# Spectra scratch read in gather order, tables built on TensorE, and LayerNorm moved ahead of the tables, in a fused long-convolution and FFN kernel

## The chip, the cores and the metric

The kernel runs on one core of a Trainium2 chip. The metric is the device time in microseconds of one execution. A kernel's figure is the median of its runs. A run of one core is called slow when it lies more than 1.5% above the fastest of the same kernel. The profile comes from one profiled execution; its span is about 2 us shorter than the run's time.

## The reference, cut to what matters

```python
x  = A_q                                    # 1 x 2048 x 640, bf16
xn = layernorm(x)
# A: a 4-tap shift convolution, then a convolution as long as the sequence, per channel
k_shift = sum over 4 taps of shifted k * shift_k
kv = k_shift * v
y  = irfft(rfft(pad(kv)) * rfft(pad(ssm_k)))[:2048] + kv * ssm_D
s  = xn * y
# B: FFN, 640 -> 1728 -> 640
g  = silu(gelu(xn @ w1 + b1) @ w2 + b2)
# the output is x plus the product s * g
```

The output is x with a small product added. The tolerance of the comparison doesn't notice if the rows of the spectra are permuted. "Correct" is therefore no argument for a change of layout here.

## The kernel before

The long convolution is a two-stage DFT written as matmuls. Stage 1 transforms the filter (kT) and kv (v_all) and stores its results in two scratch tensors in DRAM, scrK and scrU. Stage 2 reads them back in a different order, so that the second index lies on the partitions. It transforms, multiplies the two spectra, transforms back (i1) and stores into scrC. The last stage (i2) reads scrC and finishes. The FFN's matmuls are interleaved with all this. Each engine has a fixed order of instructions.

```python
scrK = dram.tile([2, P * N2, H], BF16)      # likewise scrU, scrC; P = 128, N2 = 32, H = 320 (640 bytes)

def by_h(scr):    # how stage 1 stores and how the last stage reads
    return scr.rearrange("b (p h j) d -> p b h j d", h=2, j=NJ)      # 128 is outermost
def by_n2(scr):   # how stage 2 reads
    return scr.rearrange("b (k q) d -> q b k d", q=P)                # 128 is outermost

# stage 1 store (32 for scrK, 32 for scrU), out of 4 staging buffers
nc.gpsimd.dma_start(out=by_h(scr)[:, b, :, j, :], in_=o.v[:, b])

# conv_unit(b, u), 12 units: read both spectra, then DFT, product, pair sums, inverse DFT, store
nc.sync.dma_start(out=dst.v[:, 0:n].rearrange("p (k d) -> p k d", d=H), in_=by_n2(scr)[:, b, k0:k1, :])
...
nc.vector.tensor_tensor(out=q[:, r], in0=uu..., in1=ku..., op=ALU.mult)                         # prod
nc.vector.tensor_tensor(out=q[:, :, 0, 0], in0=q[:, :, 0, 0], in1=q[:, :, 1, 1], op=ALU.subtract) # comb
nc.vector.tensor_tensor(out=q[:, :, 1, 0], in0=q[:, :, 1, 0], in1=q[:, :, 0, 1], op=ALU.add)      # comb
...
nc.gpsimd.dma_start(out=by_n2(scrC)[:, b, k0:k1, :], in_=uin.v...)                              # store

# last stage, 8 reads of 640 KB
nc.sync.dma_start(out=cb.v, in_=by_h(scrC)[:, b, :, 4 * i:4 * i + 4, :])
...
# two tables: G is W transposed by four DMA transposes; the shift weights are a broadcast DMA of 640 KB
nc.sync.dma_start_transpose(out=G[:, 4*i:4*i+4, :], in_=W[:, 4*i:4*i+4, :]...)
nc.gpsimd.dma_start(out=wb, in_=wsh_v.to_broadcast([P, 2, 4, H]))
```

Of the kernel before, what the change touches and what calls it, by code (L numbers as in the profile page):

```python
# [9 lines left out]
F32 = mybir.dt.float32  # L10
# [3 lines left out]
ALU = mybir.AluOpType  # L14
# [57 lines left out]
class Plan:  # L72
# [3 lines left out]
    def op(self, kind, engs, fn, reads=(), writes=(), mods=(), hold=(), extra=(), size=0):  # L76
        o = Op()
        o.kind, o.engs, o.fn, o.size, o.i = kind, engs.split("|"), fn, size, len(self.ops)
        o.deps, o.allocs, o.bufs, o.after = set(extra), [], [], []
# [52 lines left out]
21s -20d 6p0 16s 10s -21g 12s -24d 25s 10d -13s 14d 2a -1d -23g 25a -28p1 4d 16s 13g -31g 45d -12s 11d 2d -50p0 54d  # L132
-55p1 56a 1d -38s -22p0 13a 135p20 -93g 1d 1d -33s 149p41 2p6 1d -115d 89p0 24d -23a -130s 147p02 2p6 55d -163g 107a
-20a 3g -151p0 41s 22d 113g -112p10 2p0 -69p2 45s 20d 108a -13p43 1a 1p6 1a 1g -94d -71p2 76d -4p3 -3a 106g -161a 60p0
-57d 58d 154d -156a -47s 64p00 6p1 134d 1d 1d 1d -141p2 5a -4a 153d -152p3 1a 11p4 128p60 6p21 -5a -69p63 1a 69g -129a
134d -73p2 -64p1 139p62 4d 1d -171d -47s 214a -136p4 134g -73a 76g -154a 9p5 9a 128p60 -132a 144d 1d -12a -186s 199d
7p21 -6p02 -199s 206a -147p4 -14p2 155a -152a -83g 84p3 152g -15g -126a 3p0 -84s 82p1 -11a 161d 1d 1d 1d 1d 14d -165a
143g -150p3 5a -16a 102p62 -45p40 1a -103s 149p0 1d -46p4 44a -16p61 2p0 -160s -20p2 151d -48a 59g 212p20 -335s 158g
-24p43 6a 2d -6p6 -181p3 382p0 -202a 2a 199a 2a -225g 46p42 2p6 -130d 1d 1d 307p11 -197g 17a -11p20 73d 14d 1d -93p41
94d 1d 100d -177a -11p6 191p0 -192a -5a -111g 1d -34s 151a 88d -202d 100g 25g -17p2 101p43 94a -305d 212a -101a 178p10  # L140
18a -341s 151g 11p62 2p4 161p0 -78g -8p20 -202s1 126a -123s 125a -130d 289a -73d 91d -175p63 2p4 71a -72a 2a -24g 106d
74a 2p11 -290s 134p21 81d 1d -80p6 -180d -28d 73s 127g 75g 14d -254s 255d -85g 158a -60d 61p0 -157a 2a 52p42 104a -61d
-173p20 131a 43d 1d -173p6 174d -97g 53g -131a 176d 13d 1d -111s 188d -296p11 8p0 16p2 155p43 -163p3 15a 1g 129p61
-160a 179a 1g 116d -145p42 143d -283p1 -79s 92a 137a -145a -8a 211d 1d 1d -69a 83d -73g -149p2 209d -210a -9p0 1a 149g
-11p60 12p43 -11a 114d -252p1 150a 262s1 -400p0 -8p3 284d -185s -90a 154p61 -36p42 -135p0 143g -138a 150g -19a 36a
-154p1 6p4 113g 36g -153p5 -11a -88s 314d 61d 1g -61d -235a 12a 6a 6a -4a 397p6 -205p20 221s0 -224p03 207s0 -119d -87a
66p40 -46p02 -17a 47d -75p21 26g 207a -140p5 -64g 87s0 -24a 77d -123d 1g -46a 169d 64p6 4p0 -187d 43a -360s 379d -111g
264s2 -151d 134s1 -14a -140d 145p2 1a -155p41 -83p63 236a -3d1 -215p20 -17a 1g 37p02 75s -95a 21a -20g 64a 1p5 31s
-75g 45a -80p61 228d -227a 232d 1d 1p20 2a -235g 157d -72p40 154p6 2p0 -7a -74d 1d 1g -121d 232s1 -231d 200a -214p23
59p5 153a -154a 77d 73g -133d -24d -50d 17p00 -51p62 169d -57s -77g -5p21 140d -118a 43p41 -64d 217d0 -195g -21g 217d  # L150
-156a -92a 95a -94g 248p0 2p2 10p6 -11a 2d 8s0 -164p5 75s1 91a -9d -156a -44p03 -6p20 66p40 60s -125d -37p61 43a 1g
1p02 198d -242d 45d 115s -58a 9p5 1a -26g 165p2 4p6 11s2 -14a 5p0 -136p4 -120g 255d -98d -444s 544a 25s0 -164p5 3a
121p62 -123a -3p0 167s3 -39a 22p4 2p2 -25a -119p1 -2p6 145a -15d2 6d 1d -214g 208d 16d -152a 143p42 10d1 -145a -2a
138d 10d -157p7 148a 10p0 2p2 10p4 -39g -130a 158d 2a 1d 1d 8a -173p6 1a -5p7 178p2 4p0 1d -130s -52a -73g 264s2 -13a
5p4 -4d0 5a 1d -31g 26d -187p6 199s1 -23p20 2a 15d 17s1 1s0 -187p7 153a -176a 24a -21p4 -2p5 -24d 27a 189p02 2d -17g
-176a 192a -135p61 168s0 -167a 139p4 2p2 -1d 11p0 1a -10d 1d2 -7g 8d -135p7 144p4 4p0 2p2 -149a 148d -183p61 179a 1d1
5a 9p4 -24p20 16d 7s2 -21d 38s2 -23d 8a -190p70 191p4 15s3 -40a -170a 180d 16d -24g 55s1 1s1 -29p2 2p0 -1a 2a -196p6
-1a 182p24 -180a 190d0 -196p7 202d -15a -180d 190d -9a 1g 14d -202a 209p0 2p2 -1d 5p4 -3a -220p60 211p20 10d2 1d 2a
-11d 12p4 26s0 -39a 14a -225a 1p7 233p2 2p0 -234a 233a 5p4 -204p6 190d 15d -4a 43s0 -29s0 -217p7 193d 41s2 -231a -2a
193p24 -15g 16a -189p0 1a 11p1 1a -475s 664p6 10p2 38s1 -21s2 -31d1 1d -9d 23a -203p4 1a -43d 235d 1d 1d 9p0 4p6 37s2  # L160
-35p2 -1d -4a -211p5 217a -258d 43p4 -1a 201p02 10d0 1d -210a -17p5 232d 8p6 -23a 38s3 -37a 23a -8d 9p0 -240p4 241a
-242a 11p2 222p60 -221a 188g 35a 8d2 -220p3 211d -217p2 227d -26g 27p06 -243a 245d -223a 212g 10a -283p31 55a 239p4
5p0 -7p6 -290p2 -1a 294d -10g 15d -7d -290a 299p4 -13p0 -285d 300p6 1d -15d -213p20 1a 1p3 224d 3s3 -19p6 1d -208a
239s2 -12p0 -226g 251s0 -19p4 1d 3d -250p21 241d -240a 252p6 6p4 -257p3 252d 24s3 -18d -12g -6d 19d 1s 1d 1s -34p0
42p6 1d -16d 9p4 -263a 271d -23s -256p20 2p3 258g 12d 8s -19s -25d -235a 8d 239s 27d -2d 11p6 6p4 -5d -282a 273s 12d
-39d 5s 35s -26s -259d 246s 36d -12s 13s -6d 1s 9d 3d 1s -285p21 2p3 -1a 2a 1d 278d 1s
# [3 lines left out]
def kernel(  # L170
# [23 lines left out]
    def by_h(scr):  # L194
        return scr.rearrange("b (p h j) d -> p b h j d", h=2, j=NJ)

    def by_n2(scr):
        return scr.rearrange("b (k q) d -> q b k d", q=P)

# [18 lines left out]
    rstd = sb.tile([P, NJ], F32, name="rstd")  # L218
    dD_row = sb.tile([1, D], BF16, name="dD_row")
# [37 lines left out]

    def evict(e, out_, in_):
        (nc.scalar.copy if e == "ACT" else nc.vector.tensor_copy)(out=out_, in_=in_)  # L259
# [20 lines left out]
    wb_b, dD_b, b1r_b, b1_b, id_b, bias_b, ones_b = (Buf() for _ in range(7))  # L280
# [16 lines left out]
    op("zero", "DVE", lambda e: nc.vector.memset(xtra[:, 0:D], 0.0), writes=[z_b])  # L297
# [5 lines left out]
    def iotas(e):  # L303
        for h in range(2):
            nc.gpsimd.iota(tok[64 * h:64 * h + 64, :], pattern=[[1, NJ]], base=16 * h, channel_multiplier=32,
                           allow_small_or_imprecise_dtypes=True)
        nc.gpsimd.iota(k4[:], pattern=[[4, NK1], [4 * NK1, 2]], base=1, channel_multiplier=0,
                       allow_small_or_imprecise_dtypes=True)
# [4 lines left out]
    def small1(e):  # L313
        g = nc.gpsimd
        g.iota(pint[:, 0:1], pattern=[[0, 1]], base=0, channel_multiplier=1)
        g.iota(smi[:, 0:32], pattern=[[1, 32]], base=0, channel_multiplier=0, allow_small_or_imprecise_dtypes=True)
        g.iota(smc[:, 0:64], pattern=[[8, 2], [0, 32]], base=72, channel_multiplier=0, allow_small_or_imprecise_dtypes=True)
        g.iota(smc[:, 64:192], pattern=[[8, 2], [-8, 2], [0, 32]], base=72, channel_multiplier=0,
               allow_small_or_imprecise_dtypes=True)
        g.memset(pcol[:, 1:2], 0.0)  # L320
        for r in range(2):
            g.memset(pcol[64 * r + 32:64 * r + 64, 1:2], -8.0)

    op("small1", "POOL", small1, writes=[sm_b])

    def small2(e):
        g = nc.vector
        g.tensor_single_scalar(out=pint[:, 0:1], in_=pint[:, 0:1], scalar=31, op=ALU.bitwise_and)
        g.tensor_copy(out=pcol[:, 0:1], in_=pint[:, 0:1])
        g.tensor_scalar(out=smi[:, 0:32], in0=smi[:, 0:32], scalar1=pcol[:, 0:1], scalar2=None, op0=ALU.mult)  # L330
        g.tensor_tensor(out=smc.rearrange("p (a b) -> p a b", b=32), in0=smc.rearrange("p (a b) -> p a b", b=32),
                        in1=smi[:, None, 0:32].to_broadcast([P, 6, 32]), op=ALU.add)
        g.tensor_scalar(out=smc[:, 0:64], in0=smc[:, 0:64], scalar1=pcol[:, 1:2], scalar2=None, op0=ALU.add)
        g.tensor_copy(out=smq, in_=smc)
        g.tensor_single_scalar(out=smq, in_=smq, scalar=31, op=ALU.bitwise_and)

    op("small2", "DVE", small2, writes=[sm_b])
    op("tabsin", "ACT", lambda e: nc.scalar.activation(out=tabs[:], in_=smq, func=ACT.Sin,
# [10 lines left out]
    def small_rows(e):  # L349
        nc.scalar.dma_start(out=b1_r[:], in_=b1_v)  # L350
        nc.scalar.dma_start(out=dD_row[:], in_=dD_v)
# [5 lines left out]
    for q in range(CH):  # L357
        load(lambda e, q=q: nc.sync.dma_start(out=x01[:, q, :], in_=x_v[:, q, :]), 160, writes=[x_b[q]])
# [409 lines left out]
```

## Time and profile before

| reading | value | view |
|---|---|---|
| time | 204.97 us (204.82 to 207.04) | three runs |
| TensorE (PE) busy | 175.4 of 202.4 us | page, part 1 |
| VectorE (DVE) busy | 172.3 us | page, part 1 |
| first FFN matmul | 21.2 us | timeline |
| first read of a scratch tensor | 75.2 us | timeline |
| 16 DMA engines, 10 to 40 us | 412 to 417 GB/s, 26 per engine | page, part 2 |

Here are the busy times of the page of the kernel before: busy time, share of the span and number of instructions of each engine.

```profile
span 202.4 us, 4736 instructions
PE 175.4 (87%) x1846; PEld 88.5 (44%) x1846; DVE 172.3 (85%) x301; ACT 138.4 (68%) x206; POOL 70.6 (35%) x103
```

The page's 40 slices of the span follow; one slice is 5.06 us. Each digit is a busy share in tenths, and the last line is what the DMA engines moved.

```profile
PE   4039887689999899799999699999999999999991
DVE  7399969949999989859987978989999999467993
DMA  6999999954599988969988999686959997486664
GB/s 180 352 412 417 413 412 416 416 194 129 164 225 178 357 346 256 224 158 292 236 253 227 192 328 198 200 250 213 297 129 357 283 368 251 131 216 185 231 237 171
```

The reader should see two things. TensorE does little in the first three slices and is nearly full after slice 10. And after slice 8 the DMA engines move less than the 412 to 417 GB/s that they reached before.

The chain of waits that ended last comes next: shares of the span, first by engine, then by line.

```profile
PE 47%; issue 17%; DMA 13%; POOL 13%; DVE 5%; ACT 3%; SPq 1%; POOLq 0%; ACTq 0%; DVEq 0%
PE ps L459 18%; PE ps L491 18%; DMA scrU<-mm 9%; POOL scrK L532 6%; POOL scrU L532 4%; PE ps L638 4%; DMA x<-in_x_dram 3%; PE ps L669 3%; PE ps L691 3%; ACT mm L259 2%; POOL rstd L422 2%; DVE mm L259 1%; DVE stats L415 1%; PE ps L524 1%; ACT L495 1%
```

The DMA issues of the scratch tensors (count, KB of each, median us from issue to landing) show what a read costs when all 16 engines work on it:

```profile
mm<-scrC SPq DMA_DIRECT2D x8, 640.0 KB, 6.9
v_all<-scrU SPq DMA_DIRECT2D x10, 480.0 KB, 4.6
k_all<-scrK SPq DMA_DIRECT2D x6, 480.0 KB, 6.4
```

In the timeline (start, duration, engine, line, operation) these are the group that begins with the first FFN matmul and the first read of a scratch tensor:

```profile
21.21 7.00 PE L459 MATMUL ps<-xnT,w_sb 128*128 128x512 bf16 x25 [1.04 <-ACT xnT L259]
75.23 0.39 SPq L621 DMA_DIRECT2D xtra<-scrK  x1
```

### The profile page before, as it was taken

The numbers are of one execution on the slowest core, as the hardware profiler recorded it, in microseconds if no ns is written. First come the engines' busy times: TensorE is split into PE (matmuls) and PEld (weight loads), VectorE is DVE, ScalarE is ACT, GpSimd is POOL, SyncE is SP. The second block draws the span as 40 slices with busy tenths as digits, with TensorE's granted clock in tenths as the row PEclk, the third lists the DMA queues.
The fourth block names the chain that finished last, engine by engine and source line by source line (L and its number), as shares of the span: only waits on it lengthen the run. The fifth ranks groups of instructions, "written<-read, shape, count | busy, mean of one in ns | idle before, by whom it ended". The sixth has DMA issues, their size and how long they took to land.

```text
span 202.4 us, 4736 instructions
## 1 busy us (share of the span) xinstructions
PE 175.4 (87%) x1846; PEld 88.5 (44%) x1846; DVE 172.3 (85%) x301; ACT 138.4 (68%) x206; POOL 70.6 (35%) x103
## 2 busy tenths in 40 slices
PE   4039887689999899799999699999999999999991
PEld 1015332235555333355555234435665444566660
DVE  7399969949999989859987978989999999467993
ACT  4635467576977696599687759998987999611110
POOL 7018314068977434342545603111111101306200
PEclk9999999999999999999999969999999999999999
DMA  6999999954599988969988999686959997486664
GB/s 180 352 412 417 413 412 416 416 194 129 164 225 178 357 346 256 224 158 292 236 253 227 192 328 198 200 250 213 297 129 357 283 368 251 131 216 185 231 237 171
DMA packets 41191, 53.09 MB, mean 262 GB/s; under 512 B 12817, under 2 KB 32818, under 8 KB 41170
## 3 DMA queue, kind: packets, MB, share of 16 engines
q1 hardware_dynamic: 35376, 36.41, 61.4%
q0 software_dynamic: 5648, 16.39, 24.7%
q8 instruction: 14, 0.23, 0.4%
q14 instruction: 7, 0.06, 0.1%
q10 hardware_dynamic: 146, 0.00, 0.0%
HBM read 31.95 MB, written 18.35 MB: 249 GB/s over the span
## 4 chain that ended last, share of the span: by engine, by line
PE 47%; issue 17%; DMA 13%; POOL 13%; DVE 5%; ACT 3%; SPq 1%; POOLq 0%; ACTq 0%; DVEq 0%
PE ps L459 18%; PE ps L491 18%; DMA scrU<-mm 9%; POOL scrK L532 6%; POOL scrU L532 4%; PE ps L638 4%; DMA x<-in_x_dram 3%; PE ps L669 3%; PE ps L691 3%; ACT mm L259 2%; POOL rstd L422 2%; DVE mm L259 1%; DVE stats L415 1%; PE ps L524 1%; ACT L495 1%
## 5 line engine op out<-in xcount | busy, mean ns | idle before, releaser
L459 PE MATMUL ps<-xnT,w_sb 128*128 128x512 bf16 (+1 forms) x280 | 68.9, 392 | 4.7 <-ACT mm L259 3.5
L491 PE MATMUL ps<-w_sb,hT 128*128 128x320 bf16 x448 | 65.9, 300 | 0.3 <-ACT hT L463 0.2
L491 PEld LDWEIGHTS <-hT 128*128 128x128 bf16 x448 | 41.8, 98 | 21.6 <-issue 5.8
L259 ACT CAST mm<-ps 128x640 bf16<-128x640 f32 x52 | 34.2, 698 | 23.1 <-PE ps L524 11.2
L459 PEld LDWEIGHTS <-w_sb 128*128 128x128 bf16 (+1 forms) x280 | 25.6, 100 | 41.5 <-issue 17.1
L463 ACT ACTIVATE hT<-ps,b_f 128x512 bf16<-128x512 f32 (+1 forms) x56 | 36.7, 697 | 8.1 <-PE ps L459 8.0
L532 POOL DMA_DIRECT2D scrU<-mm x32 | 22.3, 753 | 42.7 <-ACT mm L259 37.5
L259 ACT CAST v_all<-ps 128x960 bf16<-128x960 f32 (+2 forms) x34 | 30.3, 928 | 3.8 <-PE ps L669 2.3
L495 ACT ACTIVATE sl<-ps 128x320 bf16<-128x320 f32 x32 | 14.1, 445 | 21.5 <-PE ps L491 21.2
L680 POOL DMA_DIRECT2D scrC<-v_all x12 | 9.9, 826 | 49.1 <-ACT v_all L259 26.0
L532 POOL DMA_DIRECT2D scrK<-mm x32 | 23.4, 903 | 5.7 <-ACT mm L259 5.3
L524 PE MATMUL ps<-kT,W 64*128 64x320 bf16 x64 | 8.3, 338 | 11.8 <-DMA kT<-in_kT_dram 8.1
L524 PEld LDWEIGHTS <-W 64*128 64x128 bf16 x128 | 5.3, 97 | 25.9 <-issue 19.4
L698 DVE TENSOR_TENSOR xn<-ps,xn 128x640 bf16<-128x640 f32 x16 | 12.5, 816 | 4.1 <-PE ps L691 4.0
L259 DVE CAST v_all<-ps 128x960 bf16<-128x960 f32 (+2 forms) x12 | 12.2, 1014 | 4.3 <-PE ps L669 2.2
L259 DVE CAST mm<-ps 128x640 bf16<-128x640 f32 x12 | 9.6, 817 | 6.8 <-PE ps L524 5.9
L553 DVE TENSOR_TENSOR mm<-k_all,mm 128x2560 bf16<-128x2560 bf16 x8 | 11.9, 1485 | 0.2
L550 DVE TENSOR_TENSOR mm<-k_all,mm 128x2560 bf16<-128x2560 bf16 x8 | 11.9, 1486 | 0.1
L638 PEld LDWEIGHTS <-tabs 64*32 64x32 bf16 x704 | 7.6, 90 | 9.5 <-issue 8.4
L524 PE MATMUL ps<-v_all,W 64*128 64x320 bf16 x64 | 8.1, 302 | 2.3 <-DVE v_all L557 1.5
L651 DVE TENSOR_TENSOR k_all<-v_all,xtra 128x960 bf16<-128x960 bf16 x16 | 9.7, 652 | 0.3
L651 DVE TENSOR_TENSOR kT<-v_all,k_all 128x960 bf16<-128x960 bf16 x16 | 9.6, 650 | 0.1
(86 smaller groups left out, 199.7 us busy)
## 6 DMA issues: line engine op xcount, KB each, us to landing
scrK<-mm POOLq DMA_DIRECT2D x32, 160.0 KB, 4.8
scrU<-mm POOLq DMA_DIRECT2D x32, 160.0 KB, 5.0
mm<-scrC SPq DMA_DIRECT2D x8, 640.0 KB, 6.9
v_all<-scrU SPq DMA_DIRECT2D x10, 480.0 KB, 4.6
scrC<-v_all POOLq DMA_DIRECT2D x10, 480.0 KB, 4.2
k_all<-scrK SPq DMA_DIRECT2D x6, 480.0 KB, 6.4
kT<-in_kT_dram SPq DMA_DIRECT2D x4, 640.0 KB, 9.4
v_all<-in_v_dram SPq DMA_DIRECT2D x4, 640.0 KB, 14.7
```

What stands on the lines that cost most here:

```text
L259: (nc.scalar.copy if e == "ACT" else nc.vector.tensor_copy)(out=out_, in_=in_)
L459: nc.tensor.matmul(out=ps.v[0:M, :], lhsT=w1_sb[:, ft, t, 0:M], rhs=xnT_b[c].v[:, t, :], start=(t == 0), stop=(t == DT - 1))
L463: op("gelu", "ACT", lambda e: nc.scalar.activation(out=hT_b[c].v[0:M, ft, :], in_=ps.v[0:M, :], func=ACT.Gelu_apprx_tanh, bias=b1_f[0:M, f ...
L491: nc.tensor.matmul(out=ps.v[:, 0:H], lhsT=hT_b[c].v[0:M, ft, q * P:(q + 1) * P], rhs=w2_sb[0:M, ft, h * H:(h + 1) * H], start=(ft == 0), s ...
L495: op("silu", "ACT", lambda e, h=h, ps=ps: nc.scalar.activation(out=sl.v[:, h * H:(h + 1) * H], in_=ps.v[:, 0:H], func=ACT.Silu), reads=[ps ...
L524: nc.tensor.matmul(out=ps.v[:, h, 0:H], lhsT=W[r, j, :], rhs=src[r, b, j, :], start=True, stop=True)
L532: nc.gpsimd.dma_start(out=by_h(scr)[:, b, :, j, :], in_=o.v[:, b])
L550: op("kv2", "DVE", lambda e: tt(out=kt_t, in0=win(0, 2), in1=wbc(0, 2), op=ALU.mult), reads=kb + [wb_b], writes=[kvt_b], extra=[u for b in ...
L553: op("kv2", "DVE", lambda e: tt(out=kt_t, in0=win(2, 2), in1=wbc(2, 2), op=ALU.mult), reads=kb + [wb_b], writes=[kvt_b])
L638: nc.tensor.matmul(out=ps.v[32 * g:32 * g + 32, r, i * w:(i + 1) * w], lhsT=F2[i][64 * r:64 * r + 64, :], rhs=part(src.v[64 * r:64 * r + 6 ...
L651: nc.vector.tensor_tensor(out=q[:, r], in0=uu[:, r, :, None, :].to_broadcast([P, 2, 2, w]), in1=ku[:, r, None, :, :].to_broadcast([P, 2, 2 ...
L698: nc.vector.tensor_tensor(out=xv, in0=ps.v[:, :, 0:H], in1=xv, op=ALU.mult)
```

## The change

There are four intents. The stage 2 reads shall move 3840 contiguous bytes at a time where they moved 640. Work shall go from DMA to TensorE: the transposes of G, and the broadcast of the shift weights. The first LayerNorm shall run ahead of the table building, so that the FFN starts earlier. And the stores of stage 1 shall be spread over two queues, with the pair sums partly on GpSimd (POOL).

The diff, cut to its core (the order tables, the declarations and the mechanics of the head are left out):

```diff
     def by_h(scr):
-        return scr.rearrange("b (p h j) d -> p b h j d", h=2, j=NJ)
+        return scr.rearrange("b (k c h j) d -> c k b h j d", c=4, h=2, j=NJ)
+    def put_h(scr):
+        return scr.rearrange("b (h j p) d -> p b h j d", ...)
+    def get_n2(scr):
+        return scr.rearrange("b (n c k) d -> c n b k d", n=N2, c=4)
...
-                nc.gpsimd.dma_start(out=by_h(scr)[:, b, :, j, :], in_=o.v[:, b])
-        op("s1st" + kind, "POOL", st, ...)
+                dma(e)(out=put_h(scr)[:, b, :, j, :], in_=o.v[:, b])
+        op("s1st" + kind, "POOL|SP", st, ...)
...
-            nc.sync.dma_start(out=dst.v[...], in_=by_n2(scr)[:, b, k0:k1, :])
+            nc.sync.dma_start(out=dst.v[...], in_=get_n2(scr)[:, :, b, k0:k1, :])
...
-            op("comb", "DVE", comb, ...)
+            op("comb", "DVE|POOL", comb, ...)
...
-        op("cst", "POOL", lambda e: nc.gpsimd.dma_start(out=by_n2(scrC)[:, b, k0:k1, :], ...
+        op("cst", "POOL|SP", lambda e: dma(e)(out=by_n2(scrC)[:, b, k0:k1, :], ...
...
-            op("cin", "SP", lambda e: nc.sync.dma_start(out=cb.v, in_=by_h(scrC)[:, b, :, 4 * i:4 * i + 4, :]),
+                for h in range(2):
+                    nc.sync.dma_start(out=cb.v[:, h], in_=by_h(scrC)[:, :, b, h, 4 * i:4 * i + 4, :])
...
-        op("gtr", "SP", ... nc.sync.dma_start_transpose(out=G[...], in_=W[...]))         # x4
+                nc.tensor.transpose(out=ps.v[:].bitcast(BF16)[...], in_=W[:, CH * i + j, :], identity=ident[:])  # x16
-    op("wb", "POOL", ... nc.gpsimd.dma_start(out=wb, in_=wsh_v.to_broadcast([P, 2, 4, H])))
+        op("wbm", "PE", ... nc.tensor.matmul(out=ps.v[:], lhsT=<row of ones>, rhs=wrow_f[...]))   # x5
...
+    ln_group([0, 1])                    # now ahead of the tables
+    ln_group([2, 3], (2,))
```

In `get_n2` the row number is (n c k): c steps less far than n and still stands outermost in the pattern. So c and n can't be merged into one dimension of 128, and the pattern begins with a dimension of size 4. The same holds for c and k in the new `by_h`.

## The prediction

> **What bounds the kernel now.** The page's span is 202.4 us; PE is busy 175.4 us (87%), DVE 172.3, ACT 138.4. In the chain of waits the FFN matmuls lead (L459 18%, L491 18%). PE time is lost mainly in two places. In the head, the timeline shows the first FFN matmul at 21.2 us: the third x tile lands only at 10.1 us, because kT, k and w1 loads are mixed with x; LayerNorm, transposes and evictions follow. In the slices from 5 to 40 us the 16 DMA engines are 90 to 99% busy at 412 to 417 GB/s, so 26 GB/s per engine. Then about 10 us go between 28 and 46 us (waits for scratch stores; the chain gives "DMA scrU" 9%). From 115 us on PE is nearly gapless.
>
> **What the change does.**
> 1. Head: the four x tiles go first, LayerNorm before the tables, kT and k later. By durations of the trace (x landing about 2.3 us after issue, statistics 1.1 us a tile, pow 0.7, normalise 0.44, transposes and eviction 2) FFN matmuls can start at about 11 us: minus 9 to 10 us, on the critical path.
> 2. G by 16 TensorE transposes (about 1.5 us of PE) takes four DMA transposes (5.5 us to landing) off the sync queue; shift weights by five matmuls take away a 640 KB broadcast during the saturated stretch. Worth 1 to 2 us.
> 3. Most scratch stores move to the sync queue; pair sums move from DVE (0.4 us each half) partly to POOL. Off the critical path, about zero.
> 4. Spectra reads: the 128 partitions become (4 groups x 32), with 3840-byte instead of 640-byte pieces. Fewer packets, but the DRAM side can't be merged: its outermost dimension is now 4, in the 24 reads of scrK and scrU and the 16 half reads of scrC. The Trainium skill, "DMA: Bandwidth & Descriptors", section "Why a DMA increments its semaphore by 16 and not by 1", states that a DMA runs on the largest count of engines up to 16 that divides the slowest dimension of both sides; "Rules for kernel authors" there warns of an outermost dimension under 16. So these reads run on 4 engines, the same four each time. No trace here shows it yet: in the kernel before all large transfers have 128 outermost.
>
> **Cost of 4.** The reads move 10.5 + 5.2 = 15.7 MB. On 4 engines at the measured 26 GB/s that is 151 us (estimate); one 480 KB read takes 4.7 us plus latency, per unit two. These engines also carry a sixteenth each of the later stores and transposes, about 0.67 MB, some 30 us. They can't start before all s1 stores of one half, which PE order puts at about 62 us. 62 + 151 + 30 + a tail of 6 = about 249 us. The queue, not PE, becomes the bound from about 80 us; the 10 us gained in the head are lost in waiting.
>
> **Prediction.** 250 us, range 220 to 276; faster 0.14, same 0.03, slower 0.83.
>
> **What would show it.** Right: the DMA issue table has k_all<-scrK and v_all<-scrU above 8 us to landing (6.4 and 4.6 before) and scrC reads likewise; mean DMA busy share falls to 30 to 40% in the later slices while waits for these reads lead the chain; PE share falls to about 70%; first FFN matmul at 10 to 13 us. Packets fall by some 20,000.
>
> **What would make it wrong.** If the reads still spread over 16 engines, 4 costs nothing or gains, the head's gain stays and the time is 187 to 196 us. If the four engines run faster than 26 GB/s, or start earlier, it is nearer 220. In-order blocking on the sync queue could add beyond 260.

## The result

The kernel after took 283.93 us (median of four fast runs, 281.77 to 285.09), against 205.23 us for the kernel before in the same rounds. The ratio is 1.380, with a 95% interval of 1.368 to 1.392. A ratio is the mean time of one kernel's fast runs over that of the other's of the same rounds, so it is not quite the ratio of the medians. The direction was predicted, with 250 us; the time lies above the range, which ended at 276.

The busy times, the slices (one is 7.04 us) and the chain of the page of the kernel after:

```profile
span 281.5 us, 4784 instructions
PE 200.6 (71%) x1851; PEld 95.5 (34%) x1867; DVE 167.5 (60%) x268; ACT 143.0 (51%) x215; POOL 76.7 (27%) x78
```

```profile
PE   7899979999993494567388385676494696374583
DVE  6889995797998263486438315545356235132392
DMA  7999996999949945599364522342422453222472
GB/s 200 412 415 403 292 240 152 333 327 308 276 164 119 173 123 183 174 108 118 106 197 147 193 102 103 123 156 104 153 100 100 149 211 110 102 100 100 152 262 89
```

```profile
DMA 64%; PE 19%; ACT 8%; DVE 3%; issue 3%; SPq 2%; ACTq 0%; DVEq 0%
DMA scrC<-v_all 21%; DMA mm<-scrC 16%; DMA v_all<-scrU 13%; DMA scrU<-mm 8%; PE ps L545 7%; PE ps L513 7%; ACT mm L269 4%; DMA scrK<-mm 3%; DMA k_all<-in_k_dram 2%; PE ps L690 2%; DMA x<-in_x_dram 1%; SPq L586 1%; ACT hT L517 1%; PE ps L578 1%; PE ps L495 1%
```

The first eleven slices of the DMA lines look like before. From slice 12 on the DMA engines move mostly 100 to 200 GB/s, with a floor at 100 up to the last slice but one. Their busy share is mostly 20 to 50%; from 160 to 271 us its mean is 0.35. (The digit 9 of slices 13, 14, 18 and 19 stands beside only 108 to 173 GB/s. It falls where the sync queue issues DMA transposes, between 86 and 137 us.) Yet 64% of the chain is waiting for DMA. A chain that waits for DMA engines that are mostly idle suggests that a few of them are not idle. Windows of one microsecond make this visible (columns: window, its length, busy time of PE, PEld, DVE, ACT and POOL with counts, granted TensorE clock, DMA share, GB/s):

```profile
241.00:242.00 1.00, 0.32 (x1) 0.11 (x2) 0.00 (x0) 0.00 (x0) 0.00 (x0) 1.00 0.26 100
243.00:244.00 1.00, 0.00 (x0) 0.00 (x0) 0.00 (x0) 0.00 (x0) 0.00 (x0) 0.50 0.27 102
244.00:245.00 1.00, 0.55 (x3) 0.13 (x2) 0.00 (x0) 0.00 (x0) 0.00 (x0) 0.50 0.26 100
248.00:249.00 1.00, 1.00 (x6) 0.37 (x6) 0.00 (x0) 0.00 (x0) 0.00 (x0) 0.54 0.26 100
```

Between 79 and 271 us no such window falls below a DMA share of about 0.24. Four of 16 engines are 0.25, and 100 GB/s from four engines is 25 GB/s from each, which is what each of the 16 gave in the busy head of the kernel before (412/16 = 26). So it seems that four engines always work, and the rest now and then; e4_two below tests this. The clock column shows a second loss: where TensorE had been idle for some microseconds, it is granted half its clock when it works again (0.50 from 243 to 248 us). This agrees with the Trainium skill, "TensorE: Matmul & The Clock Gate", section "Part 1: The HAM clock gate", which has the clock at half after an idle window. It is one reason why PE's busy time rose from 175.4 to 200.6 us.

The pieces of the chain in order of time (start, duration, what):

```profile
32.14 6.27 DMA scrU<-mm
...
59.57 4.35 DMA scrK<-mm
...
68.56 4.62 DMA scrK<-mm
...
138.15 11.54 DMA scrC<-v_all
...
211.77 15.00 DMA mm<-scrC
...
253.84 16.76 DMA mm<-scrC
```

The first three are waits for the stores of stage 1, of which more below. The others are reads and stores that stand in the queue of the four engines: 640 KB of scrC took 6.9 us from issue to landing before, and the two half reads now hold up the chain for 12 to 17 us. A store (138.15) suffers as well, because, if it is spread over 16 engines, a sixteenth of it lies on each of the four. Waits for such stores of scrC are even the largest single line of the chain (21%); the reads of scrC and scrU together are 29%.

The first FFN matmul and the first read of a scratch tensor, again from the timeline:

```profile
12.27 5.13 PE L513 MATMUL ps<-xnT,w_sb 128*128 128x512 bf16 x20 [0.32 <-DVE xnT L269]
75.05 0.68 SPq L673 DMA_DIRECT2D xtra<-scrK  x1
```

The head gained what was predicted: the FFN starts 8.9 us earlier. The first scratch read starts when it did before.

### The profile page after: what moved, and what is told of

It is laid out like the page before. It is cut to its first block, busy times and chain, and to the rows that moved or that the text cites. A ratio compares the mean times of both kernels' runs of the same rounds, so it can differ in the third digit from the quotient of the medians.

```text
span 281.5 us, 4784 instructions
## 1 busy us (share of the span) xinstructions
PE 200.6 (71%) x1851; PEld 95.5 (34%) x1867; DVE 167.5 (60%) x268; ACT 143.0 (51%) x215; POOL 76.7 (27%) x78
## 2 busy tenths in 40 slices
DMA packets 41242, 51.92 MB, mean 184 GB/s; under 512 B 10274, under 2 KB 32979, under 8 KB 41220
## 4 chain that ended last, share of the span: by engine, by line
DMA 64%; PE 19%; ACT 8%; DVE 3%; issue 3%; SPq 2%; ACTq 0%; DVEq 0%
DMA scrC<-v_all 21%; DMA mm<-scrC 16%; DMA v_all<-scrU 13%; DMA scrU<-mm 8%; PE ps L545 7%; PE ps L513 7%; ACT mm L269 4%; DMA scrK<-mm 3%; DMA k_all<-in_k_dram 2%; PE ps L690 2%; DMA x<-in_x_dram 1%; SPq L586 1%; ACT hT L517 1%; PE ps L578 1%; PE ps L495 1%
## 5 line engine op out<-in xcount | busy, mean ns | idle before, releaser
L545 PE MATMUL ps<-w_sb,hT 128*128 128x320 bf16 x448 | 74.7, 327 | 0.5 <-ACT hT L517 0.5
L545 PEld LDWEIGHTS <-hT 128*128 128x128 bf16 x448 | 45.4, 105 | 27.6 <-issue 6.6
L269 DVE CAST v_all<-ps 128x960 bf16<-128x960 f32 (+1 forms) x21 | 22.8, 1092 | 46.8 <-PE ps L690 29.3
L269 ACT CAST mm<-ps 128x640 bf16<-128x640 f32 (+1 forms) x57 | 36.3, 688 | 19.2 <-DMA scrU<-mm 14.0
L513 PEld LDWEIGHTS <-w_sb 128*128 128x128 bf16 (+1 forms) x280 | 26.8, 106 | 40.5 <-issue 19.6
L269 ACT CAST v_all<-ps 128x960 bf16<-128x960 f32 (+2 forms) x25 | 22.2, 898 | 27.2 <-PE ps L690 19.6
L690 PE MATMUL ps<-v_all,tabs 64*32 64x240 bf16 (+1 forms) x352 | 9.6, 291 | 30.5 <-DMA v_all<-scrU 27.9
L744 PE MATMUL ps<-mm,G 128*64 128x320 bf16 x64 | 8.7, 337 | 17.4 <-DMA mm<-scrC 17.4
L711 POOL TENSOR_TENSOR k_all<-k_all 128x480 bf16<-128x480 bf16 (+1 forms) x8 | 8.6, 1070 | 35.1 <-DVE k_all L703 17.7
L586 POOL DMA_DIRECT2D scrU<-mm x8 | 6.1, 766 | 35.3 <-ACT mm L269 27.5
L604 DVE TENSOR_TENSOR mm<-k_all,mm 128x2560 bf16<-128x2560 bf16 x8 | 11.9, 1488 | 3.2 <-DMA k_all<-in_k_dram 3.1
L551 POOL TENSOR_TENSOR xn<-xn,sl 128x640 bf16<-128x640 bf16 x7 | 9.9, 1412 | 13.2 <-ACT sl L549 13.2
```

Of the source, the lines that this page charges most:

```text
L269: (nc.scalar.copy if e == "ACT" else nc.vector.tensor_copy)(out=out_, in_=in_)
L513: nc.tensor.matmul(out=ps.v[0:M, :], lhsT=w1_sb[:, ft, t, 0:M], rhs=xnT_b[c].v[:, t, :], start=(t == 0), stop=(t == DT - 1))
L545: nc.tensor.matmul(out=ps.v[:, 0:H], lhsT=hT_b[c].v[0:M, ft, q * P:(q + 1) * P], rhs=w2_sb[0:M, ft, h * H:(h + 1) * H], start=(ft == 0), s ...
L551: op("f2m", "DVE|POOL", lambda e: eng(e).tensor_tensor(out=xn[:, j, :], in0=xn[:, j, :], in1=sl.v[:], op=ALU.mult), reads=[sl], mods=[xn_b ...
L586: dma(e)(out=put_h(scr)[:, b, :, j, :], in_=o.v[:, b])
L604: op("kv2", "DVE", lambda e: tt(out=kt_t, in0=win(0, 2), in1=wbc(0, 2), op=ALU.mult), reads=kb + [wb_b], writes=[kvt_b], extra=[u for b in ...
```

## The experiments

The kernel before itself varied from 202 to 211 us over the groups of runs that shared a chip. I therefore quote the ratio to the kernel before of the same group wherever there is one, and the median of the kernel before of that group otherwise. The theories have letters; what they stand for is said beside each.

### 1. Is it the number of DMA engines?

The first theory is that of the prediction: a DMA runs on as many engines, up to 16, as divide the slowest dimension of both its sides, so that the new reads run on four. The rival, B, says that something else in the change costs the time: the other order, the other queue, the wider pieces. The version e1_wide_wrong leaves everything and swaps the order of two dimensions in the reads, so that they merge into one of 128. It reads the same bytes in the same pieces, into the wrong partitions: it is wrong.

```diff
-  "b (k c h j) d -> c k b h j d"   /   "b (n c k) d -> c n b k d"
+  "b (k c h j) d -> (k c) b h j d" /   "b (n c k) d -> (n c) b k d"
```

> The changed kernel with the scratch reads' DRAM side walked with 32 rows outside and 4 groups inside, so that it merges to 128 rows: same bytes, same 3840-byte pieces, same number and place of DMAs, wrong partitions and so a wrong result on purpose. Theory A (the reads run on 4 of 16 engines because the outermost dimension is 4, and everything else follows from that): 187 to 197 us, scrK/scrU read below 7 us to landing, no stretch held at 100 GB/s. Rival B (the loss comes from the longer pieces themselves or from the stores that moved to the sync queue and queue up behind the reads): stays above 260 us.

It took 204.22 us (201.27 to 204.79), ratio 0.996 (0.985 to 1.007). The whole loss of 80 us is gone. The rest of the change, its gains and costs taken together, costs no time, so the rival falls. But the head's gain, which both the prediction and this expectation wanted to see, is not there either. That is the second question below.

The version e2_split4 is right by construction: each read is made as four DMAs of 32 partitions, each with 32 outermost.

```diff
-   nc.sync.dma_start(out=dst.v[:, 0:n]..., in_=get_n2(scr)[:, :, b, k0:k1, :])
+   for g in range(4):
+       nc.sync.dma_start(out=dst.v[32*g:32*g+32, 0:n]..., in_=get_n2(scr)[g:g+1, :, b, k0:k1, :])
```

> The changed kernel with each scratch read issued as 4 DMAs, one for each group of 32 partitions, so that 32 is outermost on both sides; the result stays correct. Theory A: 190 to 205 us; 120 more DMA issues of about 0.45 us on the sync queue may cost some us against the wide one. Rival B: above 260 us, since pieces, bytes and the queue are the same.

It took 212.72 us (212.01 to 215.43), ratio 1.045 (1.039 to 1.050), above the range that was written. Four DMAs on 16 engines each are 71 us faster than one on four. The extra 120 issues cost about 0.42 us each on the sync queue, which is 50 us of that queue's time. That they explain the 8.5 us by which it is slower than e1_wide_wrong is likely, but was not tested.

The version e4_two makes two DMAs of each read, with two groups of 32 partitions each. This asks which engines a DMA with a small count takes. If the two halves went to different engines, little would change. If they always take the same lowest ones, two engines carry everything.

```diff
+   for g in range(2):
+       nc.sync.dma_start(out=dst.v[64*g:64*g+64, 0:n]..., in_=get_n2(scr)[2*g:2*g+2, :, b, k0:k1, :])
```

> The changed kernel with each scratch read cut in two DMAs of two groups each, so that 2 is outermost; correct result. Theory A, with the rule that the count of engines divides the outermost dimension and that it is always the same lowest-numbered ones: 15.7 MB on 2 engines at 25.3 GB/s is 311 us, after a start at 75 us: 390 to 450 us, with stretches held at 50 GB/s. If a second DMA took other engines than the first (4 in use): 275 to 290 us as before. Rival B: within 5 us of the changed kernel.

It took 438.62 us (one look: a single run, so its state is unknown), with a span of 436.6 us. The slices of its page (one is 10.9 us) and two of its one-microsecond windows, with the columns as above:

```profile
GB/s 267 417 366 278 270 291 280 86 76 52 112 156 103 60 68 74 108 83 63 131 52 52 66 52 53 91 68 73 50 49 91 90 101 50 51 50 50 53 160 117
```

```profile
304.00:305.00 1.00, 0.00 (x0) 0.00 (x0) 0.00 (x0) 0.15 (x1) 0.00 (x0) 0.89 0.12 46
305.00:306.00 1.00, 0.00 (x0) 0.00 (x0) 0.00 (x0) 0.00 (x0) 0.00 (x0) 0.50 0.13 48
```

The floor is now about 50 GB/s and a share of 0.12 to 0.13, which is two engines of 16. Halving a DMA made it slower, because the halves don't spread. This agrees with the Trainium skill, "DMA: Bandwidth & Descriptors", section "Why a DMA increments its semaphore by 16 and not by 1", which has the lowest-numbered engines taken on this path. (The run shows that both halves share two engines, not which two.) The two spans also give the rate, if all else takes as long in both: on two engines each carries 7.86 MB of the 15.73 MB of reads, on four 3.93 MB, and the difference of 3.93 MB took 436.6 - 281.5 = 155.1 us. That is 25.3 GB/s per engine.

The version e6_before_c4 goes the other way: it takes the kernel before and gives only the reads of scrC (16 half reads, 5.24 MB) an outermost dimension of 4.

```diff
-  in_=by_h(scrC)[:, b, :, 4*i:4*i+4, :]                                   # 128 outermost
+  src = scrC.rearrange("b (k c h j) d -> c k b h j d", c=4, h=2, j=NJ)
+  for h in range(2): nc.sync.dma_start(out=cb.v[:, h], in_=src[:, :, b, h, 4*i:4*i+4, :])
```

> The kernel before, with only its eight scratch reads of the inverse stage issued as 16 half reads with the 4 groups outermost (rows permuted, so a wrong result on purpose; bytes and bytes per half read as in the changed kernel). Theory A: 5.24 MB on 4 engines at 25.4 GB/s is 52 us, half of it after the last store of that scratch at about 178 us: 212 to 232 us. If the engine count didn't matter: 203 to 208 us.

It took 234.5 us (one look; 206.85 for the kernel before in that group). The edit costs 28 us (30 against the median of that group's fast runs, 204.9); the time is a little above the range that was expected. So a third of the reads on four engines, in a kernel that is otherwise the kernel before, brings back about a third of the loss. That the shares are equal need not mean more: of some 52 us that these reads take (5.24 MB on four engines at 25.3 GB/s, an estimate), 28 to 30 show.

The version e3_oldscr undoes the layout of the scratch tensors (with it the 3840-byte pieces) and keeps the rest of the change.

```diff
-  by_h:  "b (k c h j) d -> c k b h j d"      stores: put_h     reads: get_n2
+  by_h:  "b (p h j) d -> p b h j d"          stores: by_h      reads: by_n2
```

> The changed kernel with only the scratch layout of the kernel before (640-byte pieces, 128 partitions outermost); all else of the change stays, instruction order too; correct result. Theory A: 188 to 200 us, faster than before by the 9 us that the first FFN matmul comes earlier (12.3 against 21.2 us). Rival B in the form 'the longer pieces are slow': also below 205 us; in the form 'the stores on the sync queue are slow': above 230 us.

It took 206.05 us (203.22 to 206.86), ratio 1.009 (0.999 to 1.018): the loss is gone here too, and the head's gain is missing again. Compared with e1_wide_wrong this also shows what the wider pieces are worth: e3_oldscr has 55,034 DMA packets and e1_wide_wrong 41,722, and the times are 206.05 and 204.22 us, with intervals that overlap. Wider pieces bring no gain that can be told from zero here.

Two further rivals explained part of the loss by the queue. One, Q, says that the reads are late because stores stand before them in the order of the sync queue. The version e5_stpool issues all stores of the scratch tensors from GpSimd.

```diff
-        return (nc.sync if e == "SP" else nc.gpsimd).dma_start
+        return nc.gpsimd.dma_start
```

> The changed kernel, 4-engine reads and all, with every scratch store issued from POOL as in the kernel before; correct result. Rival Q (the part beyond the predicted 250 us comes from stores waiting in the sync queue behind the slow reads): 250 to 265 us. Theory A with T (the four engines are the bound and a store costs them the same from either queue): 275 to 290 us.

It took 298.51 us (one look): 15 us more, not less, and above both of the ranges that were written. This rival falls. (The first read of a scratch tensor starts at 81.8 us here, 6.7 us later than in the kernel after.) The Trainium skill, "DMA: Bandwidth & Descriptors", section "Issuing engines are not separate DMA queues", says that the issuing engine doesn't matter for the bandwidth. The run agrees in so far as another queue freed nothing, and adds that the issue itself costs: GpSimd's busy time rose from 76.7 to 121.8 us.

The other, T, says that the eight DMA transposes of token groups 3 and 4, which stand in the same stretch, take much of the four engines' time. The version e8_petr makes them on TensorE and evicts them on ScalarE.

```diff
-  nc.sync.dma_start_transpose(out=xnT_b[c].v[:, :, q*P:(q+1)*P], in_=xn[:, j, :])       # for c = 2, 3
+  for t in range(DT): nc.tensor.transpose(out=o[:, t, :], in_=xn[:, j, t*P:(t+1)*P], identity=ident[:])
+  nc.scalar.copy(out=xnT_b[c].v[:, :, q*P:(q+1)*P], in_=...)
```

> The changed kernel, 4-engine reads and all, with the eight DMA transposes of the third and fourth token group done by TensorE and ACT instead; correct result. Theory T (the prediction's other-traffic term was too small because each DMA transpose holds all engines for 3 to 5 us, the four read engines too): 10 to 30 us less than the changed kernel, 253 to 274 us. Rival: transposes are counted by their bytes, 164 KB over 16 engines, and nothing changes: 280 to 287 us.

It took 278.68 us (one look), 5 us less than the kernel after. That lies between the two ranges that were written, so neither was right: the transposes seem to be a small part of it, as far as one run tells.

### 2. Where did the head's gain go?

With 16 engines restored, e1_wide_wrong and e3_oldscr start the FFN 9 us earlier and end when the kernel before ends. First, the windows of the kernel before and of e1_wide_wrong in three long stretches (the columns are those above; the lines of before come first). The profiled executions of e1_wide_wrong, e3_oldscr, e12_nocomb and e17_act10 count as slow, 1.5 to 2.2% above the fastest run of their kernel; those of before, e7_combdve and e9_alldve are fast. So differences of a microsecond or two between their windows prove little.

```profile
0.00:80.00 80.00, 61.83 (x356) 28.75 (x358) 68.42 (x114) 52.94 (x83) 40.07 (x67) 1.00 0.88 304
80.00:160.00 80.00, 75.72 (x1087) 38.30 (x1087) 71.20 (x132) 66.32 (x94) 22.83 (x29) 0.98 0.93 242
160.00:185.00 25.00, 25.00 (x306) 13.18 (x304) 18.83 (x33) 16.47 (x25) 4.70 (x6) 1.00 0.76 222
```

```profile
0.00:80.00 80.00, 73.53 (x418) 33.62 (x419) 68.58 (x119) 65.49 (x105) 18.86 (x29) 0.98 0.96 307
80.00:160.00 80.00, 72.62 (x1142) 35.76 (x1140) 77.25 (x110) 66.47 (x92) 38.42 (x33) 1.00 0.87 241
160.00:185.00 25.00, 21.61 (x210) 12.98 (x210) 17.74 (x19) 7.75 (x14) 14.00 (x13) 0.93 0.62 194
```

At 80 us TensorE is 11.7 us of busy time ahead in e1_wide_wrong (73.5 against 61.8, 418 matmuls against 356), and VectorE is not ahead at all (68.6 against 68.4). Then TensorE waits: it does 3.1 us less than before from 80 to 160 us and 3.4 less from 160 to 185. The first scratch read starts at 74.5 us in this version, and between 73.5 and 77.2 us in every version but e5_stpool (81.8). So the work gained in the head was FFN work, while the path through the scratch tensors begins when it did.

The first suspect, C, was that pair sums on GpSimd slow VectorE. The groups of instructions of the page (line, engine, operation, tiles, shapes, count; then busy us and mean ns of one; then idle time before it), for the products of before and of e3_oldscr:

```profile
L651 DVE TENSOR_TENSOR k_all<-v_all,xtra 128x960 bf16<-128x960 bf16 x16 | 9.7, 652 | 0.3
```

```profile
L703 DVE TENSOR_TENSOR k_all<-v_all,xtra 128x960 bf16<-128x960 bf16 x16 | 14.0, 917 | 0.3 <-DVE v_all L269 0.2
L711 POOL TENSOR_TENSOR k_all<-k_all 128x480 bf16<-128x480 bf16 (+1 forms) x8 | 8.6, 1071 | 17.2 <-DVE k_all L703 8.7
```

The same product takes 652 ns before and 917 ns when GpSimd works beside it. The Trainium skill, "SBUF — State Buffer", section "Who interferes with whom", says that a VectorE instruction with two SBUF inputs contends with a GpSimd instruction that reads SBUF. The trace agrees, and so does e9_alldve below, where these products take 649 ns. The version e7_combdve puts the pair sums back on VectorE, and e9_alldve does so with all other elementwise work that GpSimd had.

```diff
-                g = eng(e)                                     # e7: in comb
+                g = nc.vector
-        return nc.vector if e == "DVE" else nc.gpsimd          # e9: in eng
+        return nc.vector
```

> The changed kernel with the old scratch layout (the run e3_oldscr), and the 14 pair-sum steps that the change put on POOL given back to DVE at the same place in the order; correct result. Theory C (the head's 9 us are given back because a pair sum on POOL takes 2.2 to 2.9 us instead of 0.8 and, while it runs, DVE's products take 0.92 instead of 0.65 us): DVE's product lines back to 0.65 us, PE gaps from 120 to 180 us shrink by some 4 to 6 us, time 197 to 202 us against 206 for e3_oldscr. Rival D (the gain is lost in the order of the reads and in DVE's own total; POOL is only where it shows): 203 to 208 us.

> As e7_combdve, and also the seven f2 products, four final sums and three normalisations that POOL did are given to DVE; correct result. Theory C in its wider form (any elementwise work on POOL costs DVE about as much as it saves): 194 to 201 us, no slower than e7_combdve. If DVE's total is the limit instead, it is 2 to 5 us slower than e7_combdve.

The version e7_combdve took 206.86 us (205.66 to 211.2). The kernel before had a median of 206.62 us in that group, but six of its seven runs count as slow, and the one fast run took 202.28; so there is no ratio for this group. In the trace of e7_combdve the products of k_all were back at 649 ns, and the time stayed where e3_oldscr had it (206.05 us). So this theory falls as the explanation of the lost 9 us: VectorE, with the pair sums back, is no less busy in all (178.8 us against 176.2 in e3_oldscr). The version e9_alldve took 203.65 us (202.84 to 204.32), more than the one fast run of the kernel before, but 2.3 us less than e7_combdve (205.94, medians of the fast runs of the same group). VectorE got more work there and yet was busy for less time, 175.5 us. So elementwise work on GpSimd does seem to cost some 2 us. Neither outcome that was written came: it is above 194 to 201 us, and not slower than e7_combdve. This version is the base of what follows.

The next theory, E, is that VectorE's work on the scratch path after 75 us sets the end. Its rival, F, is that TensorE's total work does. Two edits take VectorE work away from e9_alldve: e11_nokv leaves out eight additions (6.6 us) before about 88 us, and e12_nocomb leaves out half of the pair sums (22, 8.3 us), which all come after 80 us. Their outputs are wrong, which doesn't matter for the times.

```diff
-  op("kv1", "DVE", lambda e: tt(out=kt_a, in0=kt_a, in1=kt_t[:, 0], op=ALU.add), ...)   # e11
+  op("kv1", "DVE", lambda e: None, ...)
-  g.tensor_tensor(out=q[:, :, 1, 0], in0=q[:, :, 1, 0], in1=q[:, :, 0, 1], op=ALU.add)  # e12
```

> As e9_alldve, with one of the adds of the shift filter left out (8 adds of 0.82 us on DVE, 6.6 us in all, done between 16 and 88 us); wrong result on purpose. Theory E: this work lies mostly ahead of the scratch path and gains 0 to 3 us: 200 to 204 us. If DVE's total over the whole kernel is the limit: 5 to 7 us less, 196 to 199 us. Rival F: 202 to 205 us.

> As e9_alldve, with the second of the two pair sums of each conv unit left out (22 of 0.40 us on DVE, 8.3 us in all, done between 80 and 170 us); wrong result on purpose. Theory E: 4 to 8 us less than e9_alldve, 195 to 200 us. Rival F: 202 to 205 us.

The version e11_nokv took 201.56 us, ratio 0.979 (0.971 to 0.988). The version e12_nocomb took 197.44 us, ratio 0.949 (0.935 to 0.963). These medians are 2 and 6 us below that of e9_alldve, which was measured in another group. Fast runs of the kernel before took 202.28 us in that group and 203.65 to 205.38 in this one, so the 2 us can't be told from the difference of the groups. The two versions share a group, and their fast runs differ by 6.1 us (medians 201.56 and 195.47). VectorE's total is nearly the same in both (169.4 and 168.7 us). So the total isn't what counts: work of VectorE late on the scratch path is worth far more than work ahead of it.

Two edits complete this to a table of two by two: e15_lesspe leaves out 28 of the FFN's matmuls (6.7 us of TensorE) in e9_alldve, and e16_lessboth does the same in e12_nocomb. Their outputs are wrong, which doesn't matter for the times.

```diff
-            for t in range(DT):
+            nt = DT if c < 2 else DT - 1
+            for t in range(nt):
```

> e9 with 28 of the first FFN's matmuls left out in token groups 3 and 4 (28 x 0.24 us = 6.7 us less TensorE work; VectorE's work unchanged; wrong on purpose). Theory E (VectorE on the scratch path sets the end): within 2 us of e9, so 201 to 204 us. Rival F (TensorE's total sets it): the 6.7 us come off, 195 to 199. Both near their limits: 2 to 4 us off, 199 to 202.

> e15 with the 22 pair sums left out as well (6.7 us less TensorE and 8.3 us less VectorE work; wrong on purpose). Theory E: like e12, 194 to 198 us. Rival F: like e15 at 195 to 199. Both near their limits: more than either alone, 189 to 194 us.

| median us of the fast runs | all TensorE work | 6.7 us of TensorE less |
|---|---|---|
| all VectorE work | 203.65 (e9_alldve) | 202.49 (e15_lesspe) |
| half the pair sums left out, 8.3 us | 195.47 (e12_nocomb, two runs) | 196.40 (e16_lessboth) |

Taking TensorE work away gains 1.2 us in the first row and loses 0.9 in the second, which is within the scatter. Taking VectorE work away gains 8.2 and 6.1 us. The 6.1 us between e15_lesspe and e16_lessboth are the safest of these differences, because these two were measured in the same group; e9_alldve and e12_nocomb were measured in other groups. Rival F falls for these versions: TensorE is 88 to 91% busy in them and yet not what the time waits for. The ratios to the kernel before are 0.994 (0.990 to 0.998) for e15_lesspe and 0.965 (0.958 to 0.973) for e16_lessboth. One of the four runs of e15_lesspe took 562.72 us at full clock. It happened once in all runs, it counts as slow, and I have no explanation for it.

### 3. Can a correct version use this?

If VectorE sets the end, moving its work elsewhere should help. Five versions tried. The version e10_actev is e9_alldve with five late PSUM evictions moved to ScalarE.

```diff
-    plan = Plan(unpack(ORDER))
+    to_act = [...]        # five evictions; ten in e17, thirteen in e18
+    plan = Plan([(i, "ACT" if i in to_act else e, s) for i, e, s in unpack(ORDER)])
```

> As e9_alldve (old scratch layout, all elementwise work on DVE), and five PSUM evictions of the last conv units moved from DVE to ACT; correct result. Theory E (without the 4-engine reads, the end is set by the scratch path, which starts with the first read at 75 us in every version, and DVE is what that path waits for in its last stretch): 198 to 202 us, 1 to 4 us below e9_alldve. Rival F (TensorE's total sets the end): no change, 202 to 205 us.

It took 203.34 us (202.07 to 206.38), ratio 0.985 (0.974 to 0.996): less gain than expected, and still the lowest ratio of the correct versions, although the intervals of these versions overlap and none is 2% faster than the kernel before.

The version e13_pesum adds to this that TensorE makes the pair sums: the inverse DFT accumulates four matmuls instead of two, with a third table that carries the minus sign. The version e14_before_pesum does the same in the kernel before.

```diff
-            for i in range(2):                                                       # 2 terms, after comb
+            for n_, (z, i, m) in enumerate(((0,0,0), (2,1,1), (1,1,0), (1,0,1))):    # 4 terms, no comb
                 ... nc.tensor.matmul(out=pc[g//2]..., lhsT=I1[z][...], rhs=q[..., r, i, m, :], start=(n_==0), stop=(n_==3))
```

> As e10_actev, and all 44 pair sums (16.6 us of DVE) replaced by two more accumulating matmuls for each product in the inverse stage on TensorE (about 6 us of PE, from 0.54 to about 1.05 us for a unit, with a third, negated table); meant to be correct. Theory E (after 75 us the scratch path waits for DVE, and the 9 us that the head gained leave TensorE room for 6 us more): 193 to 199 us. Rival F (TensorE's total is the limit): 204 to 210 us.

> The kernel before with the same replacement alone; meant to be correct. Its TensorE is nearly gapless from 115 us on, so theory E expects no gain there, 203 to 211 us; if DVE alone were the limit of the kernel before, 195 to 200 us, and the head's gain would be worth nothing.

The version e13_pesum took 202.65 us (200.17 to 206.84), ratio 0.991 (0.978 to 1.004), where 193 to 199 were expected: a miss. The version e14_before_pesum took 205.36 us, ratio 1.008 (0.998 to 1.018): no gain, as expected. VectorE's busy time fell to 158.1 us in e13_pesum and TensorE's rose to 184.7.

Two versions move more evictions: e17_act10 ten of them, e18_act13 thirteen.

> e10 with five more PSUM evictions moved from VectorE to ScalarE (about 5.4 us less VectorE work after 90 us; correct). Theory E: 1.5 to 3.5 us below e10 against the same before, so a ratio of 0.967 to 0.978. If ScalarE's order has become the limit: ratio 0.985 or more.

> e10 with eight more evictions moved (about 8.5 us less VectorE work after 90 us; correct). ScalarE then has more work than VectorE in that stretch, so no better than the version with five more: ratio 0.97 to 0.985; theory E with no limit in ScalarE would give 0.955 to 0.967.

They took 203.44 and 204.98 us, ratios 0.992 (0.982 to 1.001) and 0.993 (0.984 to 1.002). For e17_act10 this is what was written for the case that ScalarE's order is the next limit, and not what theory E without that addition wants. For e18_act13 it is no better than e17_act10, as was written, but outside both of the ranges (0.97 to 0.985 and 0.955 to 0.967). Here are the windows from 80 to 160 us of e9_alldve, e12_nocomb and e17_act10, in this order:

```profile
80.00:160.00 80.00, 73.25 (x1093) 34.88 (x1093) 74.00 (x134) 66.83 (x94) 6.35 (x8) 0.98 0.93 243
```

```profile
80.00:160.00 80.00, 75.37 (x1159) 36.82 (x1159) 72.18 (x120) 68.77 (x96) 6.36 (x8) 0.98 0.94 247
```

```profile
80.00:160.00 80.00, 73.48 (x1137) 36.48 (x1148) 70.79 (x129) 70.61 (x101) 6.38 (x8) 0.98 0.93 244
```

In e9_alldve VectorE is busy 74.0 of these 80 us. In e17_act10 it is busy 70.8 and ScalarE 70.6, both 88%, and TensorE does no more than in e9_alldve (73.5 against 73.3). In e12_nocomb TensorE does 75.4. So pair sums that are left out late on the scratch path shorten the end, and work that only changes its engine hardly does. That fits a chain of dependent steps (read, DFT, eviction, product, pair sums, inverse DFT, eviction, store) whose length counts, as well as it fits three engines that are all near their limits. The runs don't separate these two, and I leave it open.

## Why the prediction was right or wrong

The mechanism was right: the reads run on four engines, always the same ones, and become the bound from about 75 us on. The versions e1_wide_wrong, e2_split4, e4_two and e6_before_c4 show this from four sides. The signs named in advance were there: the first FFN matmul at 12.3 us (10 to 13 predicted), PE's share 71% (about 70% predicted), waits for DMA at the head of the chain, and a mean DMA share of 0.35 from 160 to 271 us (30 to 40% predicted). Two signs failed. The issue table of the page after gives no landing times for these reads, so that check could not be read. And the packets did not fall by 20,000: they went from 41,191 to 41,242, because stores that moved from GpSimd to the sync queue are counted in more packets. With all of them on GpSimd (e5_stpool) there are 25,210, which is 15,981 fewer than before.

The size was off by 34 us. The step that failed is the sum "62 + 151 + 30 + a tail of 6 = about 249 us", and in it above all the first term: the reads started at 75.1 us and not at 62. Term by term (the third is a remainder, not a measurement of its own, and the second holds if all else takes as long in e4_two as in after):

| term | predicted us | measured us | how |
|---|---|---|---|
| start of the reads | 62 | 75.1 | timeline of after |
| the reads on four engines | 151 | 155 | spans of e4_two and of after |
| other traffic on these engines | 30 | 40.5 | what is left up to 270.6, where the last read lands in the chain |
| tail | 6 | 10.9 | 281.5 - 270.6 |
| sum, the span | 249 | 281.5 | |

The profiled run took 283.25 us, 1.75 more than its span, which the prediction left out.

- The start was 13 us too early, the largest single error. I took it from the order of the matmuls on TensorE, "which PE order puts at about 62 us", as if the stores followed at once. The timeline of before had the answer: there the last filter matmul of stage 1 starts at 66.2 us, its store is issued at 69.7, and the read that waits for it stands at 75.2. In after the three are at 67.3, 67.6 to 71.1, and 75.1 us. In the chain of after, the waits at 32.1, 59.6 and 68.6 us are for stores to land (6.3, 4.4 and 4.6 us), since there are four staging buffers. The chain has the wait for the load of k (4.9 us) between them as well. The earlier FFN changed none of this: 73.5 to 77.2 us in all versions but e5_stpool.
- The reads were nearly right. The rate was 25.3 and not 26 GB/s per engine.
- The other traffic was 10 us too small, as far as the remainder tells. Its bytes were right: from 76 to 271 us, the one-microsecond windows add up to about 27.0 MB, of which 15.73 MB are the reads, so that about 11.2 MB are other traffic, 0.70 MB for each engine, and 0.67 were predicted. At 25.3 GB/s that is 28 us and not 40. So either these bytes move more slowly than the reads on the four engines, or the four lost time elsewhere; the runs don't tell which. Some 5 us went with the DMA transposes (e8_petr, one run). The rest is open.
- The tail was 5 us too small. After the last read has landed (270.6 us), the chain has 0.7 us of matmuls that use it and then 5.8 us of FFN matmuls (L545, 42 of them) that stand behind these in TensorE's order. The granted clock explains little of it: it averages 0.91 from 270.6 us to the end, after 0.56 in the 10.6 us before.
- The step "Most scratch stores move to the sync queue; pair sums move [...] about zero" held, as far as e3_oldscr and e7_combdve show: 206.05 us with the pair sums on GpSimd and 206.86 with all of them on VectorE, in two groups.
- The alternative "the time is 187 to 196 us", if the reads spread over 16 engines, was wrong, though its condition didn't arise in the kernel after. The version e1_wide_wrong, which meets it, took 204.22 us. I had put the whole gain of the head on the critical path. It isn't there: the path through the scratch tensors starts at 74.5 us in that version too, and taking VectorE work off it late is what shortened the end. That this late start is all of the reason is argued, not shown.

## What to carry to other kernels

Look at the outermost dimension of both sides of each DMA before looking at the size of its pieces: a rearrangement that puts a dimension of 4 ahead of 32 cost 80 us here, and wider pieces won nothing that could be measured. Floors in the DMA share near four or two sixteenths (0.25, 0.125) in narrow windows are the sign of it here, and a chain that waits for DMA engines that are mostly idle is the other. Before crediting an earlier start to the total, look up when the path that ends last starts, and what it waits for there. Work that isn't on that path can be 9 us ahead and end at the same time.

## What the Trainium skill lacked or had wrong

- "DMA: Bandwidth & Descriptors", section "Rules for kernel authors", advises one 128-partition transfer in place of two that each cover half of the partitions. Its reason is that both halves spread over all 16 engines. Where the 128 partitions are four groups that can't be merged on the DRAM side, the one transfer doesn't spread so, and the reverse holds: with four DMAs of 32 partitions the kernel took 212.72 us, with one 283.93. With two halves, each with a leading dimension of 2, it took 438.62. Another row of that table says to put a multiple of 16 outermost; neither says what to do where the groups can't be merged, and there splitting was the cure.
- The same page has the rule for the count of engines and says that the lowest-numbered are taken. It doesn't draw the consequence that all such DMAs queue on the same few engines, and hold up unrelated 16-engine stores (an 11.5 us wait in the chain for one store of scrC; the median 480 KB store of scrC took 4.2 us to land before), nor how this looks in a profile: floors of 100 and 50 GB/s, and DMA shares of 0.25 and 0.13.
- "SBUF — State Buffer", section "Who interferes with whom", has the contention of VectorE and GpSimd, as an exclusive lock, but no price for a mixed stream: here the mean product of k_all went from 652 to 917 ns. Giving the pair sums back to VectorE didn't move the end that could be seen, and giving back the other elementwise work too took 2.3 us off it.
- No page that I found says that the same stores are counted in more packets from the sync queue than from GpSimd: the whole kernel has 41,242 packets with most of the stores on the sync queue and 25,210 with all of them on GpSimd.
